# Fixed engine orders, an f32 load of the first v and per-head summary scores in the first stage of a sparse attention and expert kernel

## Chip, cores and metric

The kernel runs on one core of one Trainium2 chip. The metric is the device time of one execution in microseconds (us), lower is better. The same kernel was timed 3 to 11 times in each job; a difference of 2% or more counts as faster or slower.

## The reference

Attention over 4 batches of 8 heads, 768 positions, head size 64. Each position sees a window of keys nearer than 16 and one summary (maximum of k, mean of v) of each block of 32 keys. The result x (3072 by 512) goes through 8 experts, weighted by a Sinkhorn-balanced gate.

```python
k_sum = k.reshape(B, H, nb, block, D).max(axis=3)
v_sum = v.reshape(B, H, nb, block, D).mean(axis=3)
scores_l = scale * q @ k.T            # kept where abs(pos_q - pos_k) < 16
scores_s = scale * q @ k_sum.T + np.log(block)
a = softmax(concat(scores_l, scores_s)); attn = a @ concat(v, v_sum)
x = attn.transpose(0, 2, 1, 3).reshape(B * S, H * D)
P = exp(x @ w_gate - max); 8 times: normalise rows, then columns
out = sum over e of P[:, e] * (relu(x @ w1[e]) @ w2[e])
```

## The kernel before

Heads are worked in 16 pairs, four to a batch. Batch 0 comes first, in two halves of 384 positions, so that the matmuls of expert 0 (hidden layer `hps`, projection `yps`), which need x of a whole half batch, can start early. From then on they fill every hole that attention leaves on TensorE. A small scheduler in the kernel (`Plan`) orders all instructions when the kernel is built, from assumed durations; on the chip each engine then runs its queue strictly in that order. The parts that matter (... marks cuts):

```python
def load(key, fn, issue, us, deps=()):               # a load on POOL's queue, as the plan sees it
    last[0] = add("POOL", issue, fn, [last[0], *deps])
    last[1] = add("DMA", us, None, [add("RING", 0, None, [last[0]], lag=1.6), last[1]], 100.0)
    U[key] = add("LAND", 0, None, [last[1]], lag=1.0)
...
load_pair(0, "kqv")                                  # k, q, v of pair 0, cast f32 to bf16 by the DMA
...
if i >= X_BY_DMA and i % PB < PB - 1:                # pairs 12 to 14: x transposed by DMA, SyncE's queue
    U["xt", i] = add("SP", 1.5, lambda: x_dma(i), [U["no", i, 0], U["no", i, 1]], prio)
    U["x", i] = add("DMA", 1.7, None, [U["xt", i]], prio, lag=2.0)
...
gate(b, xs, 900 if b < B - 1 else 0)                 # logits; those of the last batch go first
...
def transposed():                                    # POOL waits for the DMA transposes of k and q
    nc.gpsimd.tensor_copy(out=warm[:, 0:1], in_=kT[r][0:32, 0:1])
    nc.gpsimd.tensor_copy(out=warm[:, 1:2], in_=qT[r][0:32, W:W + 1])
    ...                                              # and for the edge copies of v
last[0] = add("POOL", 0.3, transposed, [last[0], U["near", NP - 1]] + [U["kT", NP - 1, z] for z in range(2)])
load("w1n", lambda: load_w1(1), 0.85, 5.0)           # expert 1: two weights, each 2 MB read as f32
load("w2n", lambda: load_w2(1), 0.85, 5.0)           # and written as 1 MB of bf16
```

The softmax here doesn't subtract the row's maximum and nothing guards it: scores larger than these inputs give would overflow.

## Time and profile before

| what | measured |
|---|---|
| median of the timed runs | 738.96 us (738.64 to 739.21) |
| the profiled run | 741.82 us, span 740.0 us |
| PE busy | 730.5 us, 99% of the span |
| first expert matmul, profiled run | 24.84 us |
| PE's wait for x of batch 3 by DMA | 0.85 us, ending at 125.91 |

PE is TensorE and PEld its loading of weights; DVE is VectorE, ACT ScalarE, POOL GpSimd, SP SyncE. The granted clock is the share of TensorE's full clock that it was given.

The page's busy times in the kernel before (busy us, share of the span, instructions):

```profile
PE 730.5 (99%) x4300; PEld 355.8 (48%) x4300; DVE 369.2 (50%) x728; ACT 198.4 (27%) x339; POOL 95.8 (13%) x122
```

TensorE is the bound, so the time is its fixed work plus what it loses. Part of its timeline before (start, us, engine, line, operation, output and inputs, count, idle time before and what ended it). `tkq` are the transposes of k or q, `vs` the block sums of v, `hps` expert matmuls, `lp` the logits of a batch:

```profile
5.68 0.53 PE L280 MATMUL tkq<-ident,kst 128*64 128x128 bf16 x12
...
8.41 0.50 PE L332 MATMUL vs<-vx_109,m_blk 128*128 128x128 bf16 x6 [0.85 <-DMA vx_109<-in_v_dram]
...
13.86 0.57 PE L332 MATMUL vs<-vx_110,m_blk 128*128 128x128 bf16 x6 [0.88 <-DMA vx_110<-in_v_dram]
...
14.89 0.85 PE L280 MATMUL tkq<-ident,kst 128*64 128x128 bf16 x12
...
24.84 0.82 PE L206 MATMUL hps<-xT,w_347 128*128 128x384 bf16 x4
...
122.27 2.76 PE L206 MATMUL hps<-xT,w_347 128*128 128x384 bf16 x16
124.87 0.20 PE L528 MATMUL lp<-wg_bf,xT 128*128 128x8 bf16 x2
125.91 0.71 PE L528 MATMUL lp<-wg_bf,xT 128*128 128x8 bf16 x22 [0.85 <-DMA xT<-xs]
126.48 2.76 PE L206 MATMUL hps<-xT,w_347 128*128 128x384 bf16 x16
```

Two waits for v, a group of twelve transposes that takes 0.85 instead of 0.53 us after the second one (the clock had halved), and the first expert matmul at 24.84. At the bottom PE takes up batch 3's logits at 124.87 and waits 0.85 us for the last x.

The windows before show the clock (length, then busy us and instructions of PE, weight loads, DVE, ACT and POOL, then granted clock, DMA share, GB/s):

```profile
10.00:15.00 5.00, 3.85 (x80) 2.67 (x74) 4.33 (x11) 2.71 (x4) 4.73 (x7) 0.92 1.78 153
15.00:20.00 5.00, 5.00 (x62) 3.24 (x63) 3.40 (x8) 3.27 (x5) 2.63 (x5) 0.50 1.63 180
...
124.00:126.00 2.00, 1.15 (x13) 0.68 (x10) 0.00 (x0) 1.24 (x3) 0.00 (x0) 1.00 0.65 29
```

From 15 to 20 us the clock was half. (The windows view prints 1.00 where the trace holds no clock record.)

### The profile page before, as it was taken

To read this page: it belongs to the slowest core of one execution; us is meant where nothing else is said; L and a number is where in the kernel's file an instruction comes from. 1 tells how busy PE (TensorE), PEld (TensorE's weight loads), DVE (VectorE), ACT (ScalarE), POOL (GpSimd) and SP (SyncE) were. 2 spreads that over 40 slices of the span, in tenths; PEclk is the share of its full clock that TensorE was granted. 3 is DMA by queue.
4 is the path that set the end of the run, shared out by engine and by line. 5 is a ranking of instruction groups with operands and counts; after the bars stand their busy time and mean duration, and the time that the engine had idled before them with its cause. 6 is when DMAs were issued, how large, how long until landed. Compare 5 with 4: busy or idle time off the path is not lost.

```text
span 740.0 us, 10176 instructions
## 1 busy us (share of the span) xinstructions
PE 730.5 (99%) x4300; PEld 355.8 (48%) x4300; DVE 369.2 (50%) x728; ACT 198.4 (27%) x339; POOL 95.8 (13%) x122
## 2 busy tenths in 40 slices
PE   8999999999999999999999999999999999999998
PEld 4666655544444444444444444444444444444444
DVE  7789975774444444444443444444444444444443
ACT  5678665441111111111111111121121121121120
POOL 8799330040000000000000000000000000000000
PEclk8999999999999999999999999999999999999999
DMA  9999918033003300212003300222003300001213
GB/s 132 179 144 147 139 28 125 1 65 50 0 1 58 57 1 1 40 28 47 0 1 58 57 1 1 48 29 39 0 1 58 57 1 1 0 1 58 99 72 114
DMA packets 95389, 35.84 MB, mean 48 GB/s; under 512 B 76016, under 2 KB 88816, under 8 KB 95344
## 3 DMA queue, kind: packets, MB, share of 16 engines
q0 software_dynamic: 79344, 26.39, 33.1%
q1 hardware_dynamic: 15328, 8.66, 4.9%
q8 instruction: 34, 0.56, 0.3%
q10 hardware_dynamic: 672, 0.15, 0.1%
q14 instruction: 11, 0.09, 0.0%
HBM read 52.45 MB, written 6.29 MB: 79 GB/s over the span
## 4 chain that ended last, share of the span: by engine, by line
PE 89%; DVE 7%; DMA 2%; POOL 1%; issue 1%; POOLq 0%
PE hps L206 43%; PE yps L211 42%; DVE xs L501 2%; DMA xT<-xs 1%; DMA vx_110<-in_v_dram 1%; DVE em L387 1%; PE av L470 1%; PE sg L324 1%; DVE ks_104 L315 1%; DVE ks_103 L315 1%; PE ss L422 0%; DVE rc L500 0%; PE vs L332 0%; PE tx L508 0%; DVE Ve_124 L342 0%
## 5 line engine op out<-in xcount | busy, mean ns | idle before, releaser
L197 ACT ACTIVATE h<-hps 128x512 bf16<-128x512 f32 (+1 forms) x219 | 125.3, 572 | 475.1 <-PE hps L206 474.1
L211 PEld LDWEIGHTS <-h 128*128 128x128 bf16 x1544 | 150.4, 98 | 175.2
L199 DVE TENSOR_SCALAR h<-hps 128x512 bf16<-128x512 f32 (+1 forms) x181 | 123.5, 682 | 175.8 <-PE hps L206 174.5
L879 DVE SCALAR_TENSOR_TENSOR out_acc<-yps,P_sb,out_acc 128x512 f32<-128x512 f32 (+1 forms) x169 | 126.4, 748 | 165.9 <-PE yps L211 165.8
L206 PE MATMUL hps<-xT,w_347 128*128 128x384 bf16 x256 | 47.5, 326 | 0.0
L211 PE MATMUL yps<-w_501,h 128*128 128x512 bf16 x192 | 46.3, 379 | 0.0
L206 PE MATMUL hps<-xT,w_2868 128*128 128x512 bf16 x192 | 42.4, 379 | 0.0
L206 PE MATMUL hps<-xT,w_3968 128*128 128x512 bf16 x192 | 42.4, 379 | 0.0
L211 PE MATMUL yps<-w_3970,h 128*128 128x512 bf16 x192 | 42.4, 379 | 0.0
L206 PE MATMUL hps<-xT,w_5582 128*128 128x512 bf16 x192 | 42.4, 379 | 0.0
L211 PE MATMUL yps<-w_2368,h 128*128 128x512 bf16 x192 | 42.4, 379 | 0.0
L211 PE MATMUL yps<-w_2870,h 128*128 128x512 bf16 x192 | 42.4, 379 | 0.0
L206 PE MATMUL hps<-xT,w_4506 128*128 128x512 bf16 x192 | 42.4, 379 | 0.0
L211 PE MATMUL yps<-w_4508,h 128*128 128x512 bf16 x192 | 42.4, 379 | 0.0
L206 PE MATMUL hps<-xT,w_3430 128*128 128x512 bf16 x192 | 42.4, 379 | 0.0
L211 PE MATMUL yps<-w_3432,h 128*128 128x512 bf16 x192 | 42.4, 379 | 0.0
L206 PE MATMUL hps<-xT,w_5044 128*128 128x512 bf16 x192 | 42.4, 379 | 0.0
L211 PE MATMUL yps<-w_5046,h 128*128 128x512 bf16 x192 | 42.4, 379 | 0.0
L211 PE MATMUL yps<-w_5584,h 128*128 128x512 bf16 (+1 forms) x200 | 42.3, 370 | 0.0
L206 PE MATMUL hps<-xT,w_2344 128*128 128x512 bf16 x192 | 42.3, 379 | 0.0
L206 PEld LDWEIGHTS <-w_347 128*128 128x128 bf16 x256 | 23.5, 99 | 13.4
L206 PEld LDWEIGHTS <-w_3968 128*128 128x128 bf16 x192 | 18.8, 98 | 22.6
(256 smaller groups left out, 567.4 us busy)
## 6 DMA issues: line engine op xcount, KB each, us to landing
out_dram<-out_acc SPq DMA_DIRECT2D x23, 256.0 KB, 2.0
qst<-in_q_dram POOLq DMA_DIRECT2D x32, 96.0 KB, 5.6
kst<-in_k_dram POOLq DMA_DIRECT2D x24, 96.0 KB, 5.6
w_347<-in_moe_w_dram POOLq DMA_DIRECT2D x4, 256.0 KB, 7.1
w_501<-in_moe_w_dram POOLq DMA_DIRECT2D x1, 1024.0 KB, 10.5
w_2344<-in_moe_w_dram POOLq DMA_DIRECT2D x1, 1024.0 KB, 8.1
w_2368<-in_moe_w_dram POOLq DMA_DIRECT2D x1, 1024.0 KB, 14.2
w_2868<-in_moe_w_dram POOLq DMA_DIRECT2D x1, 1024.0 KB, 14.9
```

Source lines behind the costliest of these rows:

```text
L197: nc.scalar.activation(out=out, in_=in_, func=AF.Relu, bias=0.0, scale=1.0)
L199: nc.vector.tensor_scalar_max(out=out, in0=in_, scalar1=0.0)
L206: nc.tensor.matmul(hp[:, 0:n], lhsT=w1s[e][:, dk, f * 128:(f + 1) * 128], rhs=xT[:, dk, t0:t0 + n], start=(dk == 0), stop=(dk == KD - 1))
L211: nc.tensor.matmul(yp[:, d], lhsT=h[:, f, c * 128:(c + 1) * 128], rhs=w2s[e][:, f, d], start=(f == 0), stop=(f == KF - 1))
L315: nc.vector.tensor_reduce(out=ks[i % 2][:, 0, 0:24], in_=kT[r][:].rearrange("p (n w) -> p n w", w=32), axis=AX.X, op=ALU.max)
L324: nc.tensor.matmul(dst, lhsT=kT[r][p0:p0 + 64, g * 128:(g + 1) * 128], rhs=qT[r][p0:p0 + 64, g * 128 + l0:g * 128 + l1], start=True, stop= ...
L387: nc.vector.tensor_tensor(out=at["em", i][:, :, c, :], in0=at["er", i][:, :, c, W:W + 128], in1=band[:, None, None, W:W + 128].to_broadcas ...
L470: nc.tensor.matmul(av[p0:p1, o:o + n], lhsT=lhsT, rhs=rhs, start=start, stop=stop, skip_group_check=True)
L501: nc.vector.tensor_tensor(out=t.rearrange("p g j d -> p (g j) d"), in0=av[:, :, 0:D], in1=rc[:].to_broadcast([128, G, D]), op=ALU.mult)
L879: nc.vector.scalar_tensor_tensor(out=out_acc[:, t, d], in0=yp[:, d], scalar=P_sb[:, t, e:e + 1], in1=out_acc[:, t, d], op0=ALU.mult, op1=A ...
```

## The change

Its intent is to shorten the first stage. v of pair 0 no longer passes through POOL's queue; SyncE loads it as f32 and VectorE casts it. The orders of PE, VectorE and ScalarE in the first halves are written out as lists. The summary scores of first halves use the maxima of each head directly (two small matmuls) and not a spread-out copy that VectorE had to make first. Some constants move out of the prologue, and fillers (matmuls on zeros that keep PE warm) are fewer (9 for 14 at the start, single ones later). The core of the diff:

```diff
+    def follow(self, eng, units):
+        for u, d in zip(units, [None] + units):
+            u.eng = {eng: u.eng[eng]}
+            if d is not None:
+                u.deps.append(d)
...
+            if i < PB and not h:
+                for j in range(2):
+                    p = slice(64 * j, 64 * j + 64)
+                    nc.tensor.matmul(ss[32 * j:32 * j + 32, 0:HS], lhsT=ks[r][p, 0, :], rhs=rhs[p],
+                                     start=True, stop=True)
+                return
...
+        v_f32 = hpool.tile([128, 2, G, D], FP32, tag="h", name="vf32")
+        nc.sync.dma_start(out=v_f32[:]..., in_=v[0, 0:2]...)
         nc.vector.memset(zeros, 0.0)
-        keep_busy(14)
+        keep_busy(9)
...
-            hold = U["A", PB - 1, 0] if h else None
+            hold = U["xt", PB - 1, 0] if h else None
...
-        load_pair(0, "kqv")
+        load_pair(0, "kq")
+        U["vf32"] = add("LAND", 0, None, [add("RING", 0, None, [])], lag=4.8)
+        U["v", 0] = add({"DVE": 0.6}, 0,
+                        lambda: copy(U["v", 0].on, v_x[0][:, :, :, 0:D], v_f32[:]), [U["vf32"]])
...
+        plan.follow("PE", [... "T0 Q0 v0 S0 T1 Q1 s0 S1 T2 Q2 s1 A0 S2 v1 T3 A1 Q3 s2 t0 S3 v2 t1 s3 v3 A2 A3 t2 t3"])
+        plan.follow("DVE", [... "m0 V0 k1 m1 b0 q2 b1 n0 V1 m2 b2 n1 m3 x1 V2 b3 V3 n2 n3 x3"])
+        plan.follow("ACT", [... "k0 q0 X0 q1 e0 X1 k2 e1 X2 k3 q3 x0 e2 X3 e3 x2"])
...
-        plan.idle = (0.43, lambda: keep_busy(2), U["rl", 0, 0])
+        plan.idle = (0.22, lambda: keep_busy(1), U["rl", 0, 0])
```

Several assumed durations were retuned as well.

More of the change, by code (lines that the diff above doesn't have):

```diff
@@ L225 @@
         kT = [attn.tile([128, S], BF16, name=f"kT{i}") for i in range(NB)]
-        ks = [attn.tile([128, 1, 32], BF16, name=f"ks{i}") for i in range(2)]
+        ks = [attn.tile([128, 1, 32], BF16, name=f"ks{i}") for i in range(NB)]
         ksT = [attn.tile([128, 128], BF16, name=f"ksT{i}") for i in range(NB)]
@@ L314, in key_max, with key_max_split @@
             r = i % NB
-            nc.vector.tensor_reduce(out=ks[i % 2][:, 0, 0:24],
+            nc.vector.tensor_reduce(out=ks[r][:, 0, 0:24],
                                     in_=kT[r][:].rearrange("p (n w) -> p n w", w=32),
                                     axis=AX.X, op=ALU.max)
+        def key_max_split(i):
+            r = i % NB
             nc.vector.tensor_tensor(out=ksT[r][:, 0:64].rearrange("p (j n) -> p j n", j=2),
-                                    in0=ks[i % 2][:].to_broadcast([128, 2, 32]),
+                                    in0=ks[r][:].to_broadcast([128, 2, 32]),
                                     in1=own[:].to_broadcast([128, 2, 32]), op=ALU.mult)
@@ L420, in summaries @@
             r = i % NB
-            ss = at["ss", i, h] = bank(tag, "ss")
-            nc.tensor.matmul(ss[:, 0:HS], lhsT=ksT[r][:], rhs=qT[r][:, W + h * HS:W + (h + 1) * HS],
-                             start=True, stop=True)
+            ss, rhs = bank(tag, "ss"), qT[r][:, W + h * HS:W + (h + 1) * HS]
+            at["ss", i, h] = ss
+            if i < PB and not h:
[4 more added lines that the diff above has]
+                return
+            nc.tensor.matmul(ss[:, 0:HS], lhsT=ksT[r][:], rhs=rhs, start=True, stop=True)
         def summary_exp(i, h):
             if i < PB:
-                dst = at["es", i, h] = attn.tile([128, HG, 128], BF16, tag="es", name="es", bufs=2)
-                n, dst = 128, dst[:]
+                es = attn.tile([128, HG, 128], BF16, tag="es", name="es", bufs=2)
+                n = 128 if h else 64
+                dst = at["es", i, h] = es[0:n]
             else:
@@ L485, in values_h @@
             for cc in range(HG):
-                mm(0, 128, cc, 0, es[:, cc, :], V_s[i][:], n=2 * VD, stop=True)
+                mm(0, 128, cc, 0, es[:, cc, :], V_s[i][0:128 if h else 64], n=2 * VD, stop=True)
         def normalize(i, h):
@@ L570, in keep_busy @@
                 nc.tensor.matmul(t[:], lhsT=zeros[:, 0:128], rhs=zeros[:], start=True, stop=True)
+        v_f32 = hpool.tile([128, 2, G, D], FP32, tag="h", name="vf32")
+        nc.sync.dma_start(out=v_f32[:].rearrange("p j g d -> p (j g) d"),
+                          in_=v[0, 0:2].rearrange("j (g p) d -> p (j g) d", p=128))
         nc.vector.memset(zeros, 0.0)
-        keep_busy(14)
+        keep_busy(9)
         for t in v_x:
@@ L610, in constants, with summary_constants @@
                     nc.vector.memset(flat[32 * pq:32 * pq + 32, o:o + 132 * (G - 1) + 1:132], 1.0)
-            for t in V_s:
-                nc.vector.memset(t[:], 0.0)
-                nc.vector.memset(t[0:24, D:VD], 32.0)
-                nc.vector.memset(t[32:56, VD + D:2 * VD], 32.0)
-            nc.vector.tensor_copy(out=wg_bf[:], in_=wg_f32[:])
+            summary_constants(0)
+        def summary_constants(i):
+            t = V_s[i]
+            nc.vector.memset(t[:], 0.0)
+            nc.vector.memset(t[0:24, D:VD], 32.0)
+            nc.vector.memset(t[32:56, VD + D:2 * VD], 32.0)
         def edge_constants(n):
@@ L620, in edge_constants @@
                 nc.vector.memset(col_en, float(E) / float(N))
+                nc.vector.tensor_copy(out=wg_bf[:], in_=wg_f32[:])
         def value_constants(n):
@@ L633, in load @@
             last[0] = add("POOL", issue, fn, [last[0], *deps])
-            last[1] = add("DMA", us, None, [add("RING", 0, None, [last[0]], lag=1.6), last[1]], 100.0)
-            U[key] = add("LAND", 0, None, [last[1]], lag=1.0)
+            last[1] = add("DMA", us, None, [add("RING", 0, None, [last[0]], lag=1.4 if last[1] else 0.9), last[1]], 100.0)
+            U[key] = add("LAND", 0, None, [last[1]], lag=0.9)
         def load_pair(i, parts="kqv"):
@@ L640, in load_pair @@
                 if c == "v":
-                    load(("v", i), lambda: load_v(i), 0.95, 1.75,
+                    load(("v", i), lambda: load_v(i), 1.05, 1.85,
                          [U.get(("A", old, 1)), U.get(("near", old))])
@@ L644, in load_pair @@
                     h = "qr".index(c)
-                    load(("q", i, h), lambda h=h: load_qk(i, 1, h), 0.65, 0.6)
+                    load(("q", i, h), lambda h=h: load_qk(i, 1, h), 0.65, 0.65)
                 else:
@@ L648, in load_pair @@
                     load((c, i), lambda z=z: load_qk(i, z), 0.75 if i < PB else 1.65,
-                         1.1 if i < PB else 1.55, [U.get(("tr", old, z)), U.get(("tr", old, 2))])
+                         1.2 if i < PB else 1.55, [U.get(("tr", old, z)), U.get(("tr", old, 2))])
         def pair_start(i, prio):
@@ L668, in pair_start @@
                                     uses=[buf])
-            U["km", i] = add("DVE", 1.1, lambda: key_max(i), [U["kT", i, 0], U.get(("km", i - 2))] + war_q[2:], prio)
+            U["ks", i] = add("DVE", 0.95, lambda: key_max(i), [U["kT", i, 0], U.get(("km", o))], prio)
+            if i >= PB:
+                U["km", i] = add("DVE", 0.23, lambda: key_max_split(i), [U["ks", i]] + war_q[2:], prio)
             buf = Buffer("a")
@@ L672, in pair_start @@
                              [U["v", i]] + ([U.get(("A", i - NE, 1)), U["vc", i % NE]] if i >= PB else []), prio + 0.01, opens=[buf])
-            U["Vs", i] = add("DVE", 0.22 if i < PB else 0.7, lambda: block_out(i), [U["vs", i]],
+            sc = add("DVE", 0.25, lambda: summary_constants(i), [], prio - 1.0) if 0 < i < PB else None
+            U["Vs", i] = add("DVE", 0.28 if i < PB else 0.7, lambda: block_out(i), [U["vs", i], sc],
                              prio + 0.01, uses=[buf])
@@ L677, in pair_half @@
             n = PB * h + i
-            hold = U["A", PB - 1, 0] if h else None
+            hold = U["xt", PB - 1, 0] if h else None
+            if h:
+                U["km", i] = add("DVE", 0.23, lambda: key_max_split(i), [U["no", PB - 1, 0]], prio)
             tag = "a" if h else "m"
@@ L682, in pair_half @@
                                     [U["q", i, h], U["tr", i, 0], hold], prio, opens=[buf])
-            U["kT", i, 1 + h] = add({"ACT": 0.47, "DVE": 0.5}, 0,
+            U["kT", i, 1 + h] = add({"ACT": 0.48, "DVE": 0.56}, 0,
                                     lambda: tr_out(U["kT", i, 1 + h].on, i, 1, h),
@@ L689, in pair_half @@
             U["X", i, h] = add("ACT", 1.0, lambda: score_exp_h(i, h), [U["S", i, h]], prio, uses=[buf])
-            U["mk", i, h] = add("DVE", 0.78, lambda: masks_h(i, h),
+            U["mk", i, h] = add("DVE", 0.81, lambda: masks_h(i, h),
                                 [U["X", i, h], U["band"], hist("A", n - NEH)], prio)
             buf = Buffer(tag)
-            U["ss", i, h] = add("PE", 0.17, lambda: summaries(i, h, tag),
-                                [U["km", i], U["kT", i, 1 + h], hist("A", n - 2)], prio, opens=[buf])
+            U["ss", i, h] = add("PE", 0.17 if h else 0.25, lambda: summaries(i, h, tag),
+                                [U["km" if h else "ks", i], U["kT", i, 1 + h], hist("A", n - 2)], prio, opens=[buf])
             U["sx", i, h] = add("ACT", 0.46, lambda: summary_exp(i, h), [U["ss", i, h]], prio, uses=[buf])
@@ L698, in pair_half @@
                                [U["mk", i, h], U["sx", i, h], U["Vs", i]], prio, opens=[buf])
-            U["no", i, h] = add("DVE", 0.68, lambda: normalize(i, h), [U["A", i, h], hist("xt", n - 2)],
+            U["no", i, h] = add("DVE", 0.75, lambda: normalize(i, h), [U["A", i, h], hist("xt", n - 2)],
                                 prio, uses=[buf])
@@ L741, in pair_whole @@
                                    prio, opens=[buf])
-                U["no", i, h] = add("DVE", 0.68, lambda h=h: normalize(i, h),
+                U["no", i, h] = add("DVE", 0.75, lambda h=h: normalize(i, h),
                                     [U["A", i, h], U.get(("x", i - 2))], prio, uses=[buf])
@@ L785, in gate @@
             buf = Buffer("a")
-            U["lg", b] = add("PE", 0.65, lambda: logits(b), xs, prio, opens=[buf])
+            U["lg", b] = add("PE", 0.65, lambda: logits(b), xs + [U["ec", 0]], prio, opens=[buf])
             U["lo", b] = add("ACT", 0.25, lambda: logits_out(b), [U["lg", b]], prio, uses=[buf])
         last[0] = add("POOL", 1.3, None)
-        load_pair(0, "kqv")
+        load_pair(0, "kq")
+        U["vf32"] = add("LAND", 0, None, [add("RING", 0, None, [])], lag=4.8)
+        U["v", 0] = add({"DVE": 0.6}, 0,
+                        lambda: copy(U["v", 0].on, v_x[0][:, :, :, 0:D], v_f32[:]), [U["vf32"]])
         U["ident"] = last[0] = add("POOL", 0.35, ident_constant, [last[0]])
@@ L804 @@
         load("w2", lambda: load_w2(0), 0.85, 5.0)
-        add("DVE", 4.0, constants, [], -5.0)
+        add("DVE", 4.6, constants, [], -5.0)
         for i in range(PB):
@@ L809 @@
         for n in range(NE):
-            U["ec", n] = add("DVE", 0.42, lambda n=n: edge_constants(n), [U["A", PB - 1, 0]], 15 + n)
-            U["vc", n] = add("DVE", 0.5, lambda n=n: value_constants(n), [U["A", PB - 1, 0]], 15.5 + n)
+            U["ec", n] = add("DVE", 0.42, lambda n=n: edge_constants(n), [U["no", PB - 1, 0]], 15 + n)
+            U["vc", n] = add("DVE", 0.5, lambda n=n: value_constants(n), [U["no", PB - 1, 0]], 15.5 + n)
+        first = {"T": lambda i: U["tr", i, 0], "Q": lambda i: U["tr", i, 1], "k": lambda i: U["kT", i, 0],
+                 "q": lambda i: U["kT", i, 1], "v": lambda i: U["vs", i], "V": lambda i: U["Vs", i],
+                 "m": lambda i: U["ks", i], "S": lambda i: U["S", i, 0], "X": lambda i: U["X", i, 0],
+                 "b": lambda i: U["mk", i, 0], "s": lambda i: U["ss", i, 0], "e": lambda i: U["sx", i, 0],
+                 "A": lambda i: U["A", i, 0], "n": lambda i: U["no", i, 0], "t": lambda i: U["xt", i, 0],
+                 "x": lambda i: U["x", i, 0]}
+        plan.follow("PE", [first[c[0]](int(c[1])) for c in
+                           "T0 Q0 v0 S0 T1 Q1 s0 S1 T2 Q2 s1 A0 S2 v1 T3 A1 Q3 s2 t0 S3 v2 t1 s3 v3 A2 A3 t2 t3".split()])
+        plan.follow("DVE", [first[c[0]](int(c[1])) for c in
+                            "m0 V0 k1 m1 b0 q2 b1 n0 V1 m2 b2 n1 m3 x1 V2 b3 V3 n2 n3 x3".split()])
+        plan.follow("ACT", [first[c[0]](int(c[1])) for c in
+                            "k0 q0 X0 q1 e0 X1 k2 e1 X2 k3 q3 x0 e2 X3 e3 x2".split()])
         expert0(0, [U["x", i, 0] for i in range(PB)])
```

## The prediction

> **What bounds the kernel now.** TensorE. The page gives PE 730.5 us busy of a 740.0 us span. Busy time by windows: from 27 us on PE is idle for only a few us in all (longest wait: 0.85 us at 125.9, for x by DMA). So the end time is PE's fixed work plus what PE loses in the first 26 us, where batch 0's first halves run before any expert work exists. The change touches only this stage.
>
> **The stage before (timeline by engine).** 14 filler matmuls hold PE until 5.68, though k of pair 0 had landed near 5.0 (issued 1.31, 3.7 us to landing). PE then waits 0.85 us for v of pair 0, and from 12.98 to 13.86 for v of pair 1 (issued 7.44, 6.4 us to landing), at the head of its in-order queue. After that the granted clock is 0.50 from about 14.4 to 20.9, so matmuls there take about 1.5 to 2 times as long. The last x copy ends at 24.93; expert 0 starts at 24.84, then a 0.42 us gap. Real PE work up to 26.1, at full clock, is about 11.5 us (timeline's durations summed): some 14.6 us are lost, of which about 5 us, the first load, can't be had.
>
> **What changes.**
> - v of pair 0 leaves POOL's queue: 1.05 us of issue less for every later load, and its bytes move from about 2.3 us on instead of behind q. The DMA engines are near saturation from 3 us, so I count about 1 us earlier for k1 (9.2 to 8.1), v1 (13.8 to 12.6), v3 (18.9 to 17.7). Cost: a cast of about 0.6 us on DVE, and perhaps 0.3 us delay of k0 by shared DMA engines. The Trainium skill ("DMA: Bandwidth & Descriptors", Latency) gives a first byte of about 0.6 us for HWDGE, 1 us for SWDGE; here the gate weight on ACT's queue landed in 1.9 us.
> - 9 instead of 14 fillers: T0 can start at 5.1 to 5.3.
> - Summary scores from the maxima: 0.23 us per pair off the DVE chain before ss (ksT, paid later), PE 0.25 instead of 0.17.
> - V_s constants (three times 0.38 us) and the gate cast (0.18) leave the DVE prologue.
> - Fixed orders: v1's sums follow S2, so a late v1 no longer blocks ready matmuls.
>
> Walking the new lists by hand I get the last x copy near 21.7 to 22.3 instead of 24.9. About 3 us, if the clock stays up; all on the critical path, as PE is full afterwards. The moved DVE work (about 1.1 us) falls where DVE is 78% busy (25 to 45 us), and loads for pairs 4 to 6 land 4 to 7 us before use, so I expect most to be kept, minus a few tenths in new bubbles.
>
> **Clock risk.** The skill ("TensorE: Matmul & The Clock Gate", Parts 1 and 4) says a window of about 3.4 us without enough activity halves the clock, and that transposes do not count. The trace agrees in sign: 0.50 after a stretch of transposes and waits. Single fillers in planned gaps should mostly prevent it. If it goes cold anyway, about 1.5 us of the gain is lost.
>
> **Prediction:** 736.2 us, 734.8 to 737.8 in 8 of 10. Faster by over 2%: 0.01; within 2%: 0.98; slower: 0.01.
>
> **Would show it right:** T0 before 5.5; no PE wait for v; clock 1.00 through 15 to 20 us; first expert matmul at 21.7 to 22.8; the end earlier by that shift. **Wrong if:** k0 is delayed by the f32 load; the clock drops; a fixed order waits on a late operand on an in-order engine; or a larger gap opens near 125 us, giving the shift back.

## More of the kernel before

The profiled run is 2.9 us longer than the timed median.

What POOL issued before expert 1's phase, from its timeline in the kernel before:

```profile
110.23 0.79 POOL L187 DMA_DIRECT2D w_2344<-in_moe_w_dram  x1
111.00 0.91 POOL L193 DMA_DIRECT2D w_2368<-in_moe_w_dram  x1
```

The chain of waits of the same run, around the last x (start, us, what):

```profile
118.26 7.60 DMA xT<-xs
125.86 0.05 issue
125.91 0.71 PE lp L528 x22
```

The last x was issued to DMA at 118.3, some 7 us after the weights of expert 1, and landed 7.6 us later. PE had other work until 124.9, so that cost little.

## The result, and the profile after

The kernel after takes 744.37 us (median of 4 runs, 743.97 to 744.77), the kernel before 738.88 in the same rounds: ratio 1.0074, 95% interval 1.0056 to 1.0091. (The ratios are of fast runs of the same rounds; they aren't quite the ratios of the medians.) That is within 2%, but clearly slower, and outside my range.

The page's busy times after:

```profile
PE 726.4 (98%) x4233; PEld 355.9 (48%) x4302; DVE 367.5 (49%) x728; ACT 199.7 (27%) x342; POOL 90.2 (12%) x121
```

This trace lacks some records of PE (4233 matmuls for 4302 weight loads), so the two busy times of PE can't be compared.

PE's timeline after, the lines that answer to those above:

```profile
6.07 0.85 PE L287 MATMUL tkq<-ident,kst 128*64 128x128 bf16 x12 [0.79 <-DMA kst<-in_k_dram]
...
7.31 0.82 PE L342 MATMUL vs<-vx_111,m_blk 128*128 128x128 bf16 x6
...
13.94 0.52 PE L342 MATMUL vs<-vx_112,m_blk 128*128 128x128 bf16 x6
...
22.60 0.82 PE L213 MATMUL hps<-xT,w_355 128*128 128x384 bf16 x4
...
118.63 1.46 PE L213 MATMUL hps<-xT,w_355 128*128 128x384 bf16 x8
119.93 0.19 PE L545 MATMUL lp<-wg_bf,xT 128*128 128x8 bf16 x2
125.77 0.75 PE L545 MATMUL lp<-wg_bf,xT 128*128 128x8 bf16 x22 [5.65 <-DMA xT<-xs]
126.38 4.33 PE L213 MATMUL hps<-xT,w_355 128*128 128x384 bf16 x16
```

The first stage went much as predicted: PE waits for no v, and the first expert matmul comes at 22.60 where this trace's partner had 24.84. The new thing stands at the bottom. PE takes up batch 3's logits at 119.93, 5 us sooner, and waits 5.65 us. The 16 expert matmuls behind then take 4.33 us where before they took 2.76. They belong to the same half of batch 2 as the 8 just ahead of the logits (32 make up a half), so they needed nothing of what PE waited for.

The windows after:

```profile
118.00:120.00 2.00, 1.95 (x18) 1.29 (x16) 0.56 (x1) 1.08 (x2) 0.00 (x0) 1.00 1.05 180
120.00:122.00 2.00, 0.12 (x3) 0.03 (x1) 0.00 (x0) 0.49 (x1) 0.00 (x0) 1.00 1.27 164
122.00:124.00 2.00, 0.00 (x0) 0.00 (x0) 0.00 (x0) 0.00 (x0) 0.00 (x0) 0.69 1.21 195
124.00:126.00 2.00, 0.23 (x8) 0.24 (x9) 0.00 (x0) 0.00 (x0) 0.00 (x0) 0.50 1.27 207
126.00:128.00 2.00, 2.00 (x26) 1.16 (x24) 1.10 (x4) 0.35 (x2) 0.00 (x0) 0.50 0.28 46
128.00:130.00 2.00, 2.00 (x9) 1.02 (x8) 0.41 (x1) 0.84 (x2) 0.00 (x0) 0.60 0.00 0
```

All engines stand still while the DMA engines move about 200 GB/s, and the clock halves in the wait. The Trainium skill ("TensorE: Matmul & The Clock Gate", Part 1) puts such a fall and rise at about 3.4 us of little and of much activity. From the means of these windows I work out a fall at about 122.8, 2.7 us after PE stopped, and a rise at about 129.6, 3.8 us after it resumed; this agrees roughly (a second trace of the same kernel, e9 below, gives 2.7 and 4.6 us).

What POOL issued after:

```profile
112.12 0.78 POOL L194 DMA_DIRECT2D w_2434<-in_moe_w_dram  x1 [0.30 <-issue]
112.88 0.92 POOL L200 DMA_DIRECT2D w_2444<-in_moe_w_dram  x1
```

And the chain of waits after, at the same place:

```profile
113.95 11.77 DMA xT<-xs
125.77 0.75 PE lp L545 x22
```

The weights of expert 1 went out at 112.1 and 112.9, the last x at 114.0, right behind them. It landed 11.8 us after issue. So my theory, A: the weights hold up the last x on the DMA engines, and PE, whose queue is strictly in order and had been emptied of work ahead of the logits, stands still for it and then runs cold. The rivals: the x transposes are slow for a reason of their own; or the lateness of x alone, not the order on PE, sets the end.

### The profile page after: what moved, and what is told of

Read it like the earlier page. It is cut to its first block, busy times and chain, and to the rows that moved or that the text cites. A ratio compares the mean times of both kernels' runs of the same rounds, so it can differ in the third digit from the quotient of the medians.

```text
span 742.6 us, 10112 instructions
## 1 busy us (share of the span) xinstructions
PE 726.4 (98%) x4233; PEld 355.9 (48%) x4302; DVE 367.5 (49%) x728; ACT 199.7 (27%) x342; POOL 90.2 (12%) x121
## 4 chain that ended last, share of the span: by engine, by line
PE 95%; DMA 2%; DVE 1%; issue 1%; POOLq 0%
PE hps L213 44%; PE yps L218 44%; DMA xT<-xs 2%; PE sg L334 1%; PE av L487 1%; PE vs L342 1%; PE tkq L290 1%; DMA kst<-in_k_dram 1%; PE ss L439 1%; PE av L420 1%; PE tx L525 1%; PE av L426 1%; PE idle L587 0%; PE lp L545 0%; PE tkq L287 0%
## 5 line engine op out<-in xcount | busy, mean ns | idle before, releaser
L204 ACT ACTIVATE h<-hps 128x512 bf16<-128x512 f32 (+1 forms) x224 | 127.8, 571 | 478.7 <-PE hps L213 461.5
L206 DVE TENSOR_SCALAR h<-hps 128x512 bf16<-128x512 f32 (+1 forms) x176 | 120.5, 685 | 170.5 <-PE hps L213 170.2
L213 PE MATMUL hps<-xT,w_355 128*128 128x384 bf16 x256 | 49.1, 334 | 0.0
L213 PEld LDWEIGHTS <-w_355 128*128 128x128 bf16 x256 | 24.4, 101 | 14.5 <-issue 1.7
```

The source lines that it names most:

```text
L204: nc.scalar.activation(out=out, in_=in_, func=AF.Relu, bias=0.0, scale=1.0)
L206: nc.vector.tensor_scalar_max(out=out, in0=in_, scalar1=0.0)
L213: nc.tensor.matmul(hp[:, 0:n], lhsT=w1s[e][:, dk, f * 128:(f + 1) * 128], rhs=xT[:, dk, t0:t0 + n], start=(dk == 0), stop=(dk == KD - 1))
```

## The experiments

All kernels gave correct results. e1 to e8 ran on one chip, e9 to e12 on another; kernels of one chip share their runs of the kernel before.

| run | kernel | median, us | ratio to before | 95% interval |
|---|---|---|---|---|
| e1 | before, unchanged | 738.60 | 0.9993 | 0.9974 to 1.0011 |
| e2 | after, weights of expert 1 held back | 736.89 | 0.9970 | 0.9951 to 0.9989 |
| e3 | before, weights held back | 739.29 | 0.9998 | 0.9975 to 1.0021 |
| e4 | after, plan expects x later | 737.73 | 0.9979 | 0.9959 to 0.9999 |
| e5 | after, wait filled with 24 fillers | 742.44 | 1.0051 | 1.0024 to 1.0077 |
| e6 | e2 without the fixed orders | 737.77 | 0.9981 | 0.9962 to 0.9999 |
| e7 | e2 with v of pair 0 on POOL | 737.56 | 0.9978 | 0.9959 to 0.9996 |
| e8 | e2 with 14 fillers at the start | 736.43 | 0.9963 | 0.9941 to 0.9986 |
| e9 | after, unchanged | 743.49 | 1.0059 | 1.0044 to 1.0074 |
| e10 | e2 again | 736.43 | 0.9970 | 0.9953 to 0.9987 |
| e11 | e2 without the new summary scores | 737.24 | 0.9978 | 0.9962 to 0.9994 |
| e12 | e2 with v on POOL and 14 fillers | 737.67 | 0.9982 | 0.9968 to 0.9996 |

### e1: the kernel before once more

No edit.

> The kernel before, unchanged, to learn whether the trace that I predicted from is typical: its profiled run took 741.82 us, its timed runs 738.96. Theory A (the change gained about 2.2 us in the first stage and lost more at the gap near 120 to 126 us): time 738.6 to 739.3, ratio 1.000. If the new profiled run is near 739 too, I expect its trace to lack the half-clock stretch of 14 to 21 us, with the first expert matmul near 22.5 instead of 24.8; then the gain of the first stage that the two traces show was mostly an artefact of one run. If it is near 742 again, profiling costs the difference and the stretch is typical.

738.60 us, its profiled run 739.01. PE's timeline in e1:

```profile
7.34 0.53 PE L280 MATMUL tkq<-ident,kst 128*64 128x128 bf16 x12
...
23.12 0.82 PE L206 MATMUL hps<-xT,w 128*128 128x384 bf16 x4
...
122.67 0.20 PE L528 MATMUL lp<-wg_bf,xT 128*128 128x8 bf16 x2
123.12 0.71 PE L528 MATMUL lp<-wg_bf,xT 128*128 128x8 bf16 x22 [0.25 <-DMA xT<-xs]
```

What POOL issued before expert 1's phase in e1:

```profile
108.07 0.79 POOL L187 DMA_DIRECT2D w<-in_moe_w_dram  x1
108.84 0.92 POOL L193 DMA_DIRECT2D w<-in_moe_w_dram  x1
```

And from e1's chain of waits, the last x:

```profile
116.06 7.01 DMA xT<-xs
```

From 10 us on the clock stayed at 1.00, PE waited for no v, and the first expert matmul came at 23.12, although the 14 fillers ran at half clock (6.15 us for them) and the first transpose started only at 7.34. The trace that I predicted from was thus of a slower kind of run: the kernel before took 738.11 to 741.41 us in this job. Against e1 the change moved the first expert matmul by 0.5 us, not 2.2 (one trace against one).

### e2: after, with the weights of expert 1 held back

```diff
             ...
+            nc.gpsimd.tensor_copy(out=warm[:, 4:5], in_=xT[0:32, PB - 2, N - 1:N])
-        last[0] = add("POOL", 0.3, transposed, [last[0], U["near", NP - 1]] + ...)
+        last[0] = add("POOL", 0.3, transposed, [last[0], U["near", NP - 1], U["x", NP - 2]] + ...)
```

POOL reads one column of the last x that comes by DMA, and so issues the weights after it. PE's order is the same: in both traces 168 matmuls of expert 0's hidden layer start before batch 3's logits.

> The kernel after, with expert 1's weight loads held back on POOL until the DMA transposes of x of batch 3 have landed; the PE order is the same. Theory A (the third transpose of x landed 11.8 us after issue because 4 MB of weight reads were put on the same DMA engines 1 to 2 us ahead of it): landing falls to about 3.5 us, PE's wait of 5.6 us for x at 120 us goes away, the clock stays at 1.00 from 122 to 129, and the time falls by 5 to 7 us to 737 to 739. Rival B (the transposes are slow for a reason of their own, or PE's wait is set by its order): the wait stays within 1 us and the time within 743 to 745.

736.89 us: 7.5 us less than the kernel after (timed in another job; 7.1 in one job, e9 and e10), and faster than the kernel before (by less than 2%). POOL's timeline in e2:

```profile
117.23 0.78 POOL L194 DMA_DIRECT2D w<-in_moe_w_dram  x1
117.99 0.92 POOL L200 DMA_DIRECT2D w<-in_moe_w_dram  x1
```

PE's timeline in e2, around the logits of batch 3:

```profile
118.86 1.46 PE L213 MATMUL hps<-xT,w 128*128 128x384 bf16 x8
120.16 0.74 PE L545 MATMUL lp<-wg_bf,xT 128*128 128x8 bf16 x24
120.76 2.76 PE L213 MATMUL hps<-xT,w 128*128 128x384 bf16 x16
```

The transposes of x now land 2.8 to 3.6 us after issue. The logits run without a wait, the 16 expert matmuls take 2.76 us again. The x transposes are not slow of their own; theory A holds for the DMA side.

### e3: the same edit in the kernel before

The diff of e2, in the kernel before.

> The same edit in the kernel before. Theory A: only the wait of 0.85 us at 125.9 us can go, so 738.0 to 738.6 us, up to 0.9 us faster. Rival B: no change within 0.3 us.

739.29 us, ratio 0.9998: no gain that can be told, and above the 738.0 to 738.6 that I gave. The wait for x is gone in its profile, but that was only 0.25 us in the typical run e1, below what these runs resolve. Its profiled run (741.49) again had the half clock from about 16 to 23 us and its first expert matmul at 25.48. The collision was in the kernel before too (x landed 7.0 us after issue in e1); there PE still had work. The edit also moved PE's order in this kernel: 168 hidden-layer matmuls start before the logits, where the kernel before has 176.

### e4: after, with a later x in the plan

```diff
-    U["x", i] = add("DMA", 1.7, None, [U["xt", i]], prio, lag=2.0)
+    U["x", i] = add("DMA", 1.7, None, [U["xt", i]], prio, lag=9.0)
```

> The kernel after with one number of the scheduler changed: the latency that it assumes for a DMA transpose of x raised from 2 to 9 us, so that it puts ready expert matmuls ahead of batch 3's logits on PE. Loads stay as they are. If the loss is a full PE queue behind one late operand (theory A, its PE side), the wait of 5.6 us shrinks to under 2 us and the time falls to 737 to 741 us although x still lands about 8 to 12 us after issue. If DMA lateness alone sets the end (rival B), the time stays at 743 to 745.

737.73 us. The slowest of its x transposes still took 10.6 us, but PE did not wait for it:

```profile
122.61 1.46 PE L213 MATMUL hps<-xT,w 128*128 128x384 bf16 x8
123.91 5.34 PE L218 MATMUL yps<-w,h 128*128 128x512 bf16 x24
129.09 0.74 PE L545 MATMUL lp<-wg_bf,xT 128*128 128x8 bf16 x24
```

Ready expert matmuls stand ahead of the logits. So a late x is harmless in itself; it is the wrong place in PE's order that turns it into lost time. The plan had counted 1.7 and 2.0 us for a transpose that took 11.8. This rejects the second rival.

### e5: after, with the wait filled

```diff
+    if b == B - 1:
+        hot = add("PE", 0.22 * 24, lambda: keep_busy(24), xs, prio, opens=[Buffer("m")])
+        xs = xs + [hot]
```

> The kernel after with 24 filler matmuls (24 x 0.216 = 5.2 us at full clock, results unused) put on PE directly ahead of batch 3's logits, where PE waited 5.65 us; nothing else in the order changes. Theory A says that the loss has two parts, the wait itself (5.6 against 0.3 to 0.9 us before) and the clock that halves in it (16 expert matmuls at 126.4 took 4.33 us instead of 2.76, so about 1.5 us with the rest). Then the clock stays 1.00 from 122 to 130, x still lands near 125.8, and the time falls by 1.2 to 2.0 us, to 742.4 to 743.2. Rival: if the halved clock is harmless because other work hides it, the time stays at 744.0 to 744.8.

742.44 us, 1.9 us less than the kernel after had taken. PE's lines:

```profile
119.67 5.34 PE L587 MATMUL idle<-zeros 128*128 128x512 bf16 x24
124.85 0.92 PE L545 MATMUL lp<-wg_bf,xT 128*128 128x8 bf16 x24
125.63 2.76 PE L213 MATMUL hps<-xT,w 128*128 128x384 bf16 x16
```

Useless work in the wait keeps the clock up, and the matmuls after it are at full speed. About 1.6 us of the loss (4.33 less 2.76) was the cold clock; the wait itself remains. (In the profiled runs x also landed 0.7 us sooner than in the kernel after, 125.02 for 125.72, and the spans differ by the sum, 2.3 us.) One of its four runs took 744.26; the rest 741.91 to 742.75.

### e6: e2 without the fixed orders

```diff
-        first = {...}
-        plan.follow("PE", ...)
-        plan.follow("DVE", ...)
-        plan.follow("ACT", ...)
```

> The kernel of e2 (after, weights late: 736.9) without the three fixed orders of the first halves. If the fixed orders are worth something, the first expert matmul comes later than 22.9 by 0.5 us or more and the time rises to 737.4 or more. If, as I suspect from the traces, q of pair 3 waits behind A1 in the fixed order of PE (landed 14.5, issued 16.1) and the list costs as much as it saves, the first expert matmul comes at 22.4 to 23.1 and the time is 736.5 to 737.4.

737.77 us, 0.9 us more than e2, and the first expert matmul at 24.21 instead of 22.91, although its first transposes ran at full clock (0.53 us, at 6.05). Against e10 below, which was also warm by then, it is 24.21 for 20.79. My suspicion was wrong: by these traces the fixed orders help the first stage. The 0.9 us alone would not show it, as e10 spreads by more.

### e7: e2 with v of pair 0 on POOL's queue

```diff
-        v_f32 = ...; nc.sync.dma_start(...)
-        load_pair(0, "kq")
-        U["vf32"] = ...; U["v", 0] = ...
+        load_pair(0, "kqv")
```

> The kernel of e2 with v of pair 0 loaded by POOL as before (no f32 copy, no cast). Theory: the f32 load delays k of pair 0 by 1.0 to 1.5 us (landing 5.0 to 5.1 before, 6.0 and 6.5 in the two kernels with it) but brings all later loads 1.0 to 1.9 us forward. If the later loads (k and q of pair 3, v of pair 3) set the end of the first stage, undoing it makes the first expert matmul 0.5 to 1.5 us later and the time 737.4 to 738.4. If the delayed first k sets it, undoing it makes it earlier and the time 735.9 to 736.6.

737.56 us by the median, yet the profiled runs of e7 and e2 took 737.48 and 737.45, and both reached batch 3's logits at 120.16. k of pair 0 landed at 5.0 instead of 6.5, k of pair 3 at 14.5 instead of 13.6; the first expert matmul came at 22.43 instead of 22.91. Both halves of the theory are seen in the loads. But e7's clock rose at 6.85 us and e2's at 10.25 (first clock records of the traces), so what the f32 load is worth can't be told from this.

### e8: e2 with 14 fillers at the start

```diff
-        keep_busy(9)
+        keep_busy(14)
```

> The kernel of e2 with 14 instead of 9 filler matmuls at the start. They end between 5.7 and 7.4, by when the clock rises. If the start of the first transpose set the end of the first stage (a step of my prediction: 0.4 us from fewer fillers), the first expert matmul comes 0.5 to 0.9 us later than 22.9 and the time is 737.3 or more. If the later loads set it, it stays within 0.3 us of 22.9 and the time within 736.5 to 737.3.

736.43 us; the first transpose at 6.63 took 0.53 us where e2's at 6.55 took 0.85, and the first expert matmul came at 21.60. Neither expectation was met: it came sooner, with the clock already up (from 5.83 us; in e2 from 10.25). Whether the mean is better than with 9 fillers is decided by e10 below: it is not shown. The traces give a hint: with 14 fillers the clock rose at 3.9 to 7.3 us in all five, with 9 at 4.1 to 6.9 us in four and only at 10.1 to 10.7 us in the other four (e11 left out).

### e9 and e10: after, and e2, once more

No edits.

> The kernel after, unchanged, beside the other kernels of this call. Theory A: 743.9 to 744.8 again, with PE's wait for x near 120 us between 5 and 6.5 us in the profile. A profile that meets a warm PE in the first stage (as e5's did) may be earlier at the start, but then the wait is longer by as much, because x lands with the end of the weight loads.

> The kernel of e2 again (after, weights late), as the reference for small differences in this call: 736.6 to 737.3.

e9 took 743.49 us (742.55 to 744.24; 0.4 below what I expected) with a wait of 4.92 us, also just under what I expected, and 4.71 us for the 16 expert matmuls after it. e10 took 736.43 (735.40 to 738.03; I expected 736.6 to 737.3). In one call on one chip the held-back weights are worth 7.1 us.

The profiled runs of e2 and e10 are of the same kernel, and show what its spread is made of. PE's timeline in e2:

```profile
6.55 0.85 PE L287 MATMUL tkq<-ident,kst 128*64 128x128 bf16 x12 [1.27 <-DMA kst<-in_k_dram]
...
22.91 0.82 PE L213 MATMUL hps<-xT,w 128*128 128x384 bf16 x4
```

The same lines of e10:

```profile
5.82 0.53 PE L287 MATMUL tkq<-ident,kst 128*64 128x128 bf16 x12 [0.56 <-DMA kst<-in_k_dram]
...
20.79 0.82 PE L213 MATMUL hps<-xT,w 128*128 128x384 bf16 x4
```

In e2 PE was still cold at the first transposes, in e10 it was warm (its clock rose at 5.10 us); the first expert matmul differs by 2.1 us and the time by 2.05 us (737.45 and 735.40). The skill says the same of the warm-up, that its length varies from run to run (same page, Part 1). Here that spread is larger than the effects of e7, e8, e11 and e12, so I draw nothing from those but their traces.

### e11: e2 without the new summary scores

```diff
-            if i < PB and not h:
+            if False:
...                                   # the spread copy made right after the maxima, full matmuls, as before
```

> The kernel of e2 with the summary scores of the first halves done as before (both heads spread into one stationary operand on VectorE first: 0.22 us more on VectorE per pair, one matmul instead of two). If the shorter VectorE chain mattered, the first expert matmul comes 0.3 to 0.9 us later and the time is 737.2 to 738; if not, within 0.3 us of e10.

737.24 us, 0.8 above e10 but inside e10's spread. Its profiled run fell into the slow state (over 1.5% above the kernel's fastest run: 1277.31 us, mean clock 0.559), so there is no trace to decide by. Inconclusive.

### e12: a candidate

The diffs of e7 and e8 together.

> The candidate: weights late, fixed orders and summaries kept, v of pair 0 back on POOL (k of pair 0 lands at 5.0 again) and 14 fillers (clock up before the first transpose). From e7 and e8: if their effects add, the first expert matmul comes at 21.3 to 22.0 and the time is 735.6 to 736.6; if the two do the same thing (a cold first transpose), it equals e8, 736.2 to 736.8; if v on POOL costs what e7's medians hint, 736.9 to 737.6.

737.67 us, the worst of the expected ranges or beyond. All 14 fillers ran cold in the profiled run, the first transpose started at 7.34 and the first expert matmul at 23.55; k of pair 3 landed at 15.3. The effects are not seen to add. The best kernels stay e2 (10 runs over e2 and e10, medians 736.89 and 736.43) and e8 (736.43), 2 to 3 us below the kernel before.

## Why the prediction was wrong

**The step that failed** is "all on the critical path, as PE is full afterwards", with "minus a few tenths in new bubbles". PE was full because expert matmuls happened to stand ahead of a late operand. Its premise, "the change touches only this stage", failed with it: the new order of the one list reached as far as batch 3. I had named a larger gap near 125 us as what could give the shift back, but gave it no size and no cause. Measured, from where PE waits for the last x to the end:

| term, e1 to after | us |
|---|---|
| last x landed, 116.06 + 7.01 to 113.95 + 11.77 | +2.65 |
| 16 expert matmuls behind the logits at half clock, 2.76 to 4.33 | +1.6 |
| 8 expert matmuls that now stand behind the logits and not ahead of them (1.32 us in the chain of waits after) | +1.3 |
| sum | +5.5 |
| spans, 737.2 to 742.6 | +5.4 |

PE stood waiting for this x in both runs, so the 0.5 us of the first stage is in none of the terms: the wait swallowed it.

- Why did the wait grow by 5.4 us (0.25 to 5.65)? About half is PE's side: it came to the logits 2.7 us sooner (122.67 to 119.93). Of this the faster start is 0.5 us, and 1.3 us is that 168 hidden-layer matmuls start before the logits and not 176; the remaining 0.9 us is in part smaller waits (from the first expert matmul to the logits PE is idle for 0.7 us in e2, which has the order of after, and for 1.1 us in e1). The other half is the DMA side: x was issued 2.1 us sooner and yet landed 2.65 us later. Before, x was issued 7.2 to 7.3 us after the second weight load. After, POOL issued the weights 4.0 us later (108.07 to 112.12) and x followed the second by 1.1 us.
- e2 (hold back the weights) and e4 (let PE do other work first) each remove the loss alone, so both conditions were needed. Shown. How the DMA engines shared their time so that x had to wait so long is not shown. Which part of the diff moved the order of PE and POOL is not shown either: e6, e7, e8, e11 and e12 each undo one part or two, but all with the weights held back, which by itself moves the order (e3).
- Size of the gain in the first stage: "about 3 us" held against the trace I read (24.84 to 22.60), but that trace was of a slow kind of run. The hint was on the table: its profiled run took 741.82, the timed ones 738.96. Against e1 the gain was 0.5 us. That e2, without the collision, took 736.89 and so lies in my range does not bear out the first-stage figure: in the traces of e1 and e2 the first expert matmul moved by 0.2 us only. The same kernel in e10 had it 2.1 us sooner, so no single pair of traces gives this gain well.
- Right: no wait for v, clock 1.00 from 15 to 20 us, the first expert matmul at 22.60 (I said 21.7 to 22.8), later loads earlier (k of pair 1 landed at 7.5 for my 8.1, v of pair 1 at 12.0 for 12.6, v of pair 3 at 17.3 for 17.7). The cast took 0.71 us for my 0.6.
- Wrong in the first stage: I had the first transpose before 5.5; it came at 6.07. The f32 load delayed k of pair 0 by 1.0 us (landing 5.0 to 6.0), not 0.3, and with 9 fillers PE was cold at it (0.85 us instead of 0.53). That "9 instead of 14 fillers" gain time was not borne out: e8 lost nothing with 14.
- The fixed orders gain: without them the first expert matmul came 1.3 us later than in e2 and 3.4 us later than in e10 (e6; one trace each).

## What to carry to other kernels

When PE is full only because ready work stands ahead of a late operand, work out how long that stock of work lasts before counting a gain upstream as a gain at the end: here PE came to the late operand 2.7 us sooner, and only 0.5 us of that was the faster start. Where a program orders all work from assumed durations, compare the whole order before and after a change, not only the stage that was edited. Put an operand whose landing is uncertain behind ready work in an in-order queue, and keep bulk prefetch off the DMA engines until small transfers that somebody waits for have landed. Before reading a trace closely, compare the profiled run's time with the timed ones; if they differ by more than the effect sought, look at another trace first.

## What the Trainium skill lacked or had wrong

- "DMA: Bandwidth & Descriptors" (Queues, rings and completion order) says that each DMA engine takes turns between the queues that have work. Read simply, a small transfer on another queue should not wait for the end of a bulk load. Here DMA transposes of x on SyncE's queue took 2.8 to 3.6 us with nothing or a few copies of 10 KB beside them (e2), 7.0 us when issued 7.2 us behind two loads of 2 MB (f32 read) on POOL's queue (e1) and 11.8 us when issued 1.1 us behind them (after). The page has no figure for this case.
- The same page has no figure for what a load on a second queue costs one that is issued just after it: with a 384 KB f32 load on SyncE's queue the first k on POOL's landed at 5.5 to 6.5 us (nine traces), without it at 5.0 to 5.3 us (five), and the small gate load on ACT's took 3.7 to 3.9 us instead of 1.9 to 2.0.
- "TensorE: Matmul & The Clock Gate" (Part 1) gives a clock of one half, and of 13/16 for three and more busy cores of a die. One profiled run of this one-core kernel stayed at about 0.56 from about 10 us to its end and took 1277.31 us (e11). No page has such a state.
- The same part gives no share of activity at which the clock falls. In the kernel before it fell at 14.16 us, after 3.41 us in which PE was busy for 2.26 and paused for no more than 0.88 at a time; in e3 at 16.05 us, after 1.97 us of 3.41 (longest pause 1.16). In e10 it stayed up over such stretches with 2.80 us busy. Each of the four cold stretches after the start (before, e3, after, e9) lasted 6.83 us by the clock records. That transposes do not count as activity (Part 4), which the prediction used, is neither shown nor refuted by a run here.
